# An FFT and two MLPs on one core: the start is folded by VectorE alone, weights are made one unit ahead, rows of tiles lie 1664 bytes apart

## The chip, the core and the metric

One core of a Trainium2 chip runs the program. The metric is the time of one execution on the device in microseconds; lower is better. It is given as the median of a few runs, and one execution more was recorded by the hardware profiler.

## What is computed

The reference takes `x` (4 batches, 3072 tokens, 256 columns), makes the real part of a 2D Fourier transform of each batch, and passes every token through two MLPs:

```python
X = np.fft.fft(np.fft.fft(x, axis=1), axis=2).real
h = X @ w_in;  g = np.maximum(0.01 * h, h);  y = g @ w_out          # 256 -> 2048 -> 256
xk, xr = mixes of y and of y one token earlier, by mu_k and mu_r
k = np.maximum(xk @ w_k, 0);  out = sigmoid(xr @ w_r) * (k * k @ w_v)  # 256 -> 1024 -> 256
```

The weights arrive as 64-bit floats.

## The kernel before

**Two parts.** The first part makes `y`, the second (from about 950 us on) makes the output. Matmuls of precision run as three: each operand is split into a high and a low part, and high x high, high x low and low x high are added (`hi_lo`, line 80: ScalarE copies the high part, VectorE subtracts to get the low part).

**Folding and the transform along tokens.** The transform along the columns is taken into `w_in` (below), so that only the tokens are transformed. Rows of `x` come in six groups of 128 partitions with four mirrored rows each (`xl`, 512 KB a group). Sums and differences of the mirrored rows and columns (`full`, lines 187 to 197, for batch 0; DMAs that add, `second`, and `fin` for batches 1 to 3) give `plus` and `minus`, which hold four operands: "Pe", "Qe", "Po" and "Qo". Each is multiplied with two tables (`fft_a`, line 233, with the first three groups, `fft_b`, line 245, with the last three); between the two halves ScalarE copies the first half's sum (`ev`), and from both VectorE makes two of the four classes of frequencies A1, A2, G1, G2. A class has 386 or 384 columns; its P part is even and its Q part odd in the columns. One column apart from the others (column 128) goes the same way in small: `c_fold`, `c_a`, `c_b`; its row goes out to DRAM (`cd`) and comes back spread over all partitions (`load_c`, tile `cb`).

**Units.** For each batch, class and 128 columns of `w_in`'s 2048 there is a unit, 16 units a class, 4 x 4 x 16 = 256 in all. `mm_a` (line 476) multiplies the P part with the even weights `weh`, `wel`; `ev_a` (484) on VectorE adds the row `cb` times `w128`; `mm_b` (489) adds the Q part with `woh`, `wol`; VectorE makes `d`, ScalarE the two leaky results `g`, ScalarE and VectorE split them into `gh` and `gl`, and `outmm` (496) does twelve matmuls with `w_out`. `step` (536) issues `mm_b` of this unit, `mm_a` of the next, and `outmm` of the unit two before. After `step`, the functions that the loop calls are queued behind it on their engines: the order of the program text is the order of each engine's queue.

**Weights.** A quarter-megaword piece of 64-bit weights (256 columns of `w_in`, or 256 rows of `w_out`) is turned into 32-bit floats with a correction in three steps (`f64_steps`, line 95): ScalarE `h`, VectorE two operations, VectorE one more, ScalarE `lf`, and a product on GpSimd (`r`). `w_in_mm` (310) multiplies a piece of `w_in` with cosine and sine matrices, `w_in_split` (324) splits it (ScalarE `wh`, VectorE `wl`), `w_in_row` (333) makes `w128`. For `w_out` the steps are named `wout[q][0]` (those three), `[1]` (ScalarE copy, GpSimd sum) and `[2]` (VectorE `uol`). In the kernel before, pieces 0 to 2 of `w_in` and 0 and 1 of `w_out` are taken up before the first unit, and the others in `boot` (457) while units 0 to 11 run, each two or three units before it is used.

**The start.** Lines 394 to 454 are the order before the first unit. Groups 0, 1, 3 and 4 are folded by VectorE and groups 2 and 5 by GpSimd. All loads are issued from SyncE's queue (SP) in this order: `w_in` 0, `ce`, `so`, row groups 0, 2, 1, `w_in` 1, five small loads, row groups 5, 3, 4, tables a, b, `w_out` 0, tables a2, b2, further weights.

Of the kernel before, what the change touches and what calls it, by code (L numbers as in the profile page):

```python
# [55 lines left out]
def fft_mlp_kernel(ctx, tc, xa, xb, x7, x8, x87, tb, alt, ce, so, mu, w_in, w_out, w_k, w_v, w_r, out):  # L56
# [104 lines left out]
    def fold_ops(b):  # L161
# [5 lines left out]
        def first(g, p=None):  # L167
            if b == 0:
                t = st[g] = p.tile([P, 2, 2, D], F32, tag="xl", bufs=2 if p is fft else 4, name=f"xl{b}_{g}")
                Q.dma_start(t[:, 0], xa[b, g])  # L170
                Q.dma_start(t[:, 1], xb[b, g, :, :, 0:D])
            else:
                eo[g] = fft.tile([P, 2, 2, P], F32, tag="eo", bufs=2, name=f"eo{b}_{g}")
                st[g] = fft.tile([P, 2, D], F32, tag="xl", bufs=2, name=f"xl{b}_{g}")
                Q.dma_start(eo[g][:, 0], xa[b, g, :, :, 0:P])
                Q.dma_start(st[g], xa[b, g])


        def second(g):
            E = eo[g][:, 0]  # L180
            G.dma_start(E, xa[b, g, :, :, P:D], accum_op=ALU.add)
            G.dma_start(st[g], xb[b, g, :, :, P:P + D], accum_op=ALU.add)
            G.dma_start(E, xb[b, g, :, :, 0:P], accum_op=ALU.add)
            G.dma_start(E, xb[b, g, :, :, P:D], accum_op=ALU.add)


        def full(g, E, tags):
            t = st[g].rearrange("p z o d -> p (z o) d")
            e = work.tile([P, 4, P], F32, tag=tags[0][0], bufs=tags[0][1], name=f"fe{g}")
            o = work.tile([P, 4, P], F32, tag=tags[1][0], bufs=tags[1][1], name=f"fo{g}")  # L190
            eo[g] = work.tile([P, 2, 2, P], F32, tag=tags[2][0], bufs=tags[2][1], name=f"eo{b}_{g}")
            E.tensor_tensor(e, t[:, :, :P], t[:, :, P:], op=ALU.add)  # L192
            E.tensor_tensor(o, t[:, :, :P], t[:, :, P:], op=ALU.subtract)  # L193
            E.tensor_tensor(eo[g][:, 0], e[:, 0:2], e[:, 2:4], op=ALU.add)  # L194
            E.tensor_tensor(eo[g][:, 1], o[:, 0:2], o[:, 2:4], op=ALU.subtract)
            fin(g, 2, E)
            fin(g, 3, E)
# [21 lines left out]

        return first, second, full, fin, load7, fold7  # L220
# [24 lines left out]
    def fft_b(b, kind, ps, ev):
# [5 lines left out]
        y1 = pqp.tile([P, JP], F32, tag=nm, bufs=3, name=f"c{b}{kind}1")  # L251
        y2 = pqp.tile([P, JP], F32, tag=nm, bufs=3, name=f"c{b}{kind}2")
        act_copy(y1, ps[:, :JP])
        if nm == "P":
            V.scalar_tensor_tensor(y2, ev, 2.0, y1, op0=ALU.mult, op1=ALU.subtract)
        else:
            V.scalar_tensor_tensor(y2, ev, -2.0, y1, op0=ALU.mult, op1=ALU.add)

            for k, y in ((k1, y1), (k2, y2)):
                if b == 0 and k == A1:  # L260
                    act_copy(y[0:1], cs0[0:1, 0])
                else:
                    Q.dma_start(y[0:1], cd[b, k:k + 1])
# [80 lines left out]
    def w_out_load(q, ahead=False):  # L344
        if q < 8:
            st = load_f64(w_out[q * 256:(q + 1) * 256].rearrange("(k p) d -> p k d", p=P), 2, D, ahead)
            s = slice(2 * q % HF, 2 * q % HF + 2)
            wout[q] = f64_hi_lo(uoh[2 * q // HF][:, s], uol[2 * q // HF][:, s], st, 2, D, *((work, "gl") if q < 3 else (stage, "f")))


    def c_fold():
# [56 lines left out]
    next_tabs(2)
    w_out_load(0)
    next_tabs(2)  # L410
    w_in_load(2, True)
    w_out_load(1, True)
    w_in_load(3)
    w_out_load(2)
    w_in_parts(0)
# [19 lines left out]
    w_in_split(1)
    wout[0][0]()
    pe = fft_a(0, "Pe")
    ca = c_a(c8p, "a", True)
    w_in_row(1)
    w_in_parts(2)  # L440
    fft_b(0, "Pe", *pe)
    wout[0][1]()
    cs0 = c_b(c8p, "b", A1, *ca)
    cur_c = load_c(0, A1)
    wout[1][0]()
    qe = fft_a(0, "Qe")
    wout[0][2]()
# [559 lines left out]
```

## Time and profile before

| | us |
|---|---|
| median of 3 runs | 1550.82 |
| lowest and highest | 1550.01, 1552.66 |
| the profiled execution | 1551.64 |
| its span, first to last instruction | 1549.8 |
| TensorE (PE) busy | 1518.3 |
| VectorE (DVE) busy | 1065.6 |
| ScalarE (ACT) busy | 917.5 |
| GpSimd (POOL) busy | 162.0 |

The engines work side by side, each through its own queue, and wait for one another by semaphores. The chain of waits that ended last is followed back from the end of the program; what stands in it sets the time. TensorE's clock is gated: the profile lists the granted clock (1.0 is 2.4 GHz, 0.5 is 1.2 GHz).

### The profile page before, as it was taken

The numbers are of one execution on the slowest core, as the hardware profiler recorded it, in microseconds if no ns is written. First come the engines' busy times: TensorE is split into PE (matmuls) and PEld (weight loads), VectorE is DVE, ScalarE is ACT, GpSimd is POOL, SyncE is SP. The second block draws the span as 40 slices with busy tenths as digits, with TensorE's granted clock in tenths as the row PEclk, the third lists the DMA queues.
The fourth block names the chain that finished last, engine by engine and source line by source line (L and its number), as shares of the span: only waits on it lengthen the run. The fifth ranks groups of instructions, "written<-read, shape, count | busy, mean of one in ns | idle before, by whom it ended". The sixth has DMA issues, their size and how long they took to land.

```text
span 1549.8 us, 22458 instructions
## 1 busy us (share of the span) xinstructions
PE 1518.3 (98%) x8418; PEld 1472.9 (95%) x8418; DVE 1065.6 (69%) x1783; ACT 917.5 (59%) x1761; POOL 162.0 (10%) x144
## 2 busy tenths in 40 slices
PE   5999999999999999999999999999999999999999
PEld 2789998999998999999999999999999999999998
DVE  7876775566766567666677775777777766777775
ACT  2565655556565555555566566666666666666664
POOL 4333210031200122100010000000000000000000
PEclk8999999999999999999999999999999999999999
DMA  7426312363312353212311001111111111111100
GB/s 246 154 73 138 77 31 80 106 136 63 75 26 90 105 117 53 56 42 74 107 53 28 19 21 42 41 52 50 48 48 41 42 42 41 42 42 42 42 21 32
DMA packets 74296, 102.12 MB, mean 66 GB/s; under 512 B 10798, under 2 KB 53822, under 8 KB 74186
## 3 DMA queue, kind: packets, MB, share of 16 engines
q1 hardware_dynamic: 54538, 88.85, 18.3%
q0 software_dynamic: 19648, 11.83, 5.9%
q8 instruction: 66, 1.08, 0.3%
q14 instruction: 44, 0.36, 0.1%
HBM read 72.83 MB, written 27.83 MB: 65 GB/s over the span
## 4 chain that ended last, share of the span: by engine, by line
PE 94%; DVE 2%; DMA 2%; issue 1%; ACT 1%; SPq 0%; POOL 0%; DVEq 0%; POOLq 0%; ACTq 0%
PE o L505 33%; PE kps L815 17%; PE v L856 17%; PE ps L494 8%; PE ps L482 8%; PE rps L864 4%; DMA xl<-in_xb 2%; PE wps L320 1%; PE cps L362 0%; DMA eo<-in_xa 0%; PE cps L371 0%; DVE fe L192 0%; DVE fo L193 0%; DVE ev L487 0%; DVE eo L194 0%
## 5 line engine op out<-in xcount | busy, mean ns | idle before, releaser
L546 DVE SCALAR_TENSOR_TENSOR d<-ev,ps 128x384 f32<-128x384 f32 (+1 forms) x256 | 141.8, 554 | 214.1 <-PE ps L494 213.9
L75 ACT ACTIVATE gh<-g 128x768 fp32r<-128x768 f32 (+1 forms) x256 | 216.6, 846 | 78.8 <-PE o L505 76.5
L819 ACT ACTIVATE rl<-kps 128x384 f32<-128x384 f32 x254 | 125.0, 492 | 218.5 <-PE kps L815 218.4
L526 DVE TENSOR_TENSOR gl<-g,gh 128x768 fp32r<-128x768 f32 (+1 forms) x256 | 250.8, 980 | 1.5 <-ACT gh L75 1.0
L78 ACT ACTIVATE g<-ps 128x384 f32<-128x384 f32 (+1 forms) x256 | 126.1, 492 | 211.3 <-DVE d L546 211.1
L820 DVE SCALAR_TENSOR_TENSOR k<-kps,rl 128x384 f32<-128x384 f32 x254 | 141.6, 558 | 137.8 <-ACT rl L819 133.9
L505 PE MATMUL o<-gl,uoh 128*128 128x384 f32 (+1 forms) x1024 | 229.9, 339 | 0.0
L505 PE MATMUL o<-gh,uoh 128*128 128x384 f32 (+1 forms) x1024 | 229.4, 338 | 0.0
L505 PE MATMUL o<-gh,uol 128*128 128x384 f32 (+1 forms) x1024 | 229.0, 337 | 0.0
L505 PEld LDWEIGHTS o<-gl,uoh 128*128 128x128 f32 x1024 | 184.0, 188 | 0.0
L505 PEld LDWEIGHTS o<-gh,uol 128*128 128x128 f32 x1024 | 184.0, 188 | 0.0
L505 PEld LDWEIGHTS o<-gh,uoh 128*128 128x128 f32 x1024 | 183.8, 188 | 0.0
L487 DVE SCALAR_TENSOR_TENSOR ev<-cb,w,ps 128x384 f32<-128x384 f32 (+1 forms) x256 | 157.2, 614 | 0.0
L82 DVE TENSOR_TENSOR k2l<-k,k2h 128x384 fp32r<-128x384 f32 x254 | 139.5, 549 | 0.4 <-ACT k2h L75 0.4
L856 PE MATMUL v<-k2h,wvh 128*128 128x384 f32 x510 | 135.1, 336 | 0.0
L856 PE MATMUL v<-k2h,wvl 128*128 128x384 f32 x510 | 135.1, 336 | 0.0
L856 PE MATMUL v<-k2l,wvh 128*128 128x384 f32 x510 | 135.1, 336 | 0.0
L78 ACT ACTIVATE g<-d 128x384 f32<-128x384 f32 (+1 forms) x256 | 132.9, 519 | 0.0
L75 ACT ACTIVATE k2h<-k 128x384 fp32r<-128x384 f32 x254 | 131.2, 517 | 0.0
L815 PE MATMUL kps<-mh,wkh 128*128 128x384 f32 x508 | 129.6, 336 | 1.3 <-ACT mh L75 0.7
L815 PE MATMUL kps<-ml,wkh 128*128 128x384 f32 x508 | 129.5, 336 | 0.0
L815 PE MATMUL kps<-mh,wkl 128*128 128x384 f32 x508 | 129.4, 336 | 0.0
(295 smaller groups left out, 2497.5 us busy)
## 6 DMA issues: line engine op xcount, KB each, us to landing
out_dram<-o SPq DMA_DIRECT2D x31, 384.0 KB
y<-yo SPq DMA_DIRECT2D x24, 384.0 KB
xl<-in_xa SPq DMA_DIRECT2D x24, 256.0 KB
xa<-y SPq DMA_DIRECT2D x16, 384.0 KB
tab_a<-in_tb SPq DMA_DIRECT2D x8, 579.0 KB
tab_b<-in_tb SPq DMA_DIRECT2D x8, 579.0 KB
tab_c<-in_tb SPq DMA_DIRECT2D x8, 579.0 KB
tab_d<-in_tb SPq DMA_DIRECT2D x8, 579.0 KB
```

The costliest lines, as they stand in the source:

```text
L75: A.activation(o, i, ACTF.Copy)
L78: A.activation(o, i, ACTF.Prelu, alpha=0.01)
L82: V.tensor_tensor(lo, src, hi.bitcast(F32), op=ALU.subtract)
L482: T.matmul(x["ps"][:, :n], l[:, f], r[:, :n], start=(i == 0), stop=(i == 2))
L487: V.scalar_tensor_tensor(x["ev"][:, :n], x["cb"][:, :n], w128[:, u:u + 1], x["ps"][:, :n], op0=ALU.mult, op1=ALU.add)
L505: T.matmul(po[s][h][:, :n], w[:, u % HF, h * P:(h + 1) * P], g[:, s, :n], start=(u == 0 and i == 0), stop=(u == NF - 1 and i == 2))
L526: V.tensor_tensor(gl[:, :, :n], x["g"][:, :, :n], x["gh"][:, :, :n].bitcast(F32), op=ALU.subtract)
L546: V.scalar_tensor_tensor(d[:, :n], x["ev"][:, :n], 2.0, x["ps"][:, :n], op0=ALU.mult, op1=ALU.subtract)
L815: T.matmul(ps[:, :J], w[:, k, sl], x[:, k], start=(i == 0), stop=(i == 5))
L819: A.activation(r, ps[:, :J], ACTF.Relu)
L820: V.scalar_tensor_tensor(k2, ps[:, :J], 0.0, r, op0=ALU.max, op1=ALU.mult)
L856: T.matmul(vps[m][:, :J], w[:, f, m * P:(m + 1) * P], x, start=(f == 0 and i == 0), stop=(f == NK - 1 and i == 2))
```

## The change

- Batch 0 is folded by VectorE alone, each group in three parts: `even0` (sums, and `plus` for "Pe"), `odd0` (differences, and `minus` for "Qe"), and `rest0` ("Po" and "Qo"), which runs after unit 1. The differences overwrite the rows in place. A group comes with one load (`x0`) instead of two.
- The order of loads: row groups 0 to 2, table a, row groups 3 to 5, table b, `w_in` 0, tables a2 and b2, `w_in` 1, `w_out` 0. Six small loads are issued from ScalarE's queue. Four `memset`s go from VectorE to GpSimd, and `c_b`'s write to DRAM goes from GpSimd's queue to SyncE's.
- Before the first unit only piece 0 of `w_in` is made ready, and piece 1 between `mm_a` and `mm_b` of unit 0. `boot` makes the others over units 0 to 15, each one unit before use; `w_in_row` stands inside `step`, between `mm_b` and the next `mm_a`. The halves of A2 that come from "Pe" and "Qe" (`later`) are made after unit 0. `fft_a` of "Po" goes from unit 2 to unit 5, the small `c_a` and `c_b` one unit later.
- Tiles with rows of 386 columns (1544 bytes) get rows of `PJ` = 416 columns (1664 bytes), of which 386 or 384 are used.

```diff
+PJ = 416
...
+        def even0(g):
+            if g % 3 == 0:
+                sums.append(work.tile([P, 3, 2, P], F32, tag="yo", bufs=2, name=f"sums{g}"))
+            t, E = st[g], sums[g // 3][:, g % 3]
+            e = work.tile([P, 4, P], F32, tag="g", bufs=2, name=f"fe{g}")
+            V.tensor_tensor(e, t[:, :, :P], t[:, :, P:], op=ALU.add)
+            V.tensor_tensor(E, e[:, 0:2], e[:, 2:4], op=ALU.add)
+            V.tensor_tensor(plus[:, g, 0], E[:, 0], E[:, 1], op=ALU.add)
+
+        def odd0(g):
+            t = st[g]
+            o = work.tile([P, 4, P], F32, tag="gh", bufs=2, name=f"fo{g}")
+            O = eo[g] = t[:, 0].rearrange("p (o n) -> p o n", o=2)
+            V.tensor_tensor(o, t[:, :, :P], t[:, :, P:], op=ALU.subtract)
+            V.tensor_tensor(O, o[:, 0:2], o[:, 2:4], op=ALU.subtract)
+            V.tensor_tensor(minus[:, g, 1], O[:, 0], O[:, 1], op=ALU.subtract)
+
+        def rest0(g):
+            if g % 3 == 0:
+                E = sums[g // 3]
+                V.tensor_tensor(minus[:, g:g + 3, 0], E[:, :, 0], E[:, :, 1], op=ALU.subtract)
+            V.tensor_tensor(plus[:, g, 1], eo[g][:, 0], eo[g][:, 1], op=ALU.add)
+            if g == 0:
+                fold7o()
...
-    V.memset(one0.bitcast(F32), 0.0)
-    V.memset(one0[0:1].bitcast(F32), 1.0)
-    V.memset(altt, 0.0)
-    V.memset(e7p, 0.0)
+    G.memset(altt, 0.0)
+    G.memset(e7p, 0.0)
+    G.memset(one0.bitcast(F32), 0.0)
+    G.memset(one0[0:1].bitcast(F32), 1.0)
...
-        G.dma_start(cd[:, k1:k1 + 2], cs)
-        return cs
+
+        def other():
+            V.scalar_tensor_tensor(cs[:, 1], ev, 2.0, ps[:4, :JP], op0=ALU.mult, op1=ALU.subtract)
+            Q.dma_start(cd[:, k1:k1 + 2], cs)
+        return cs, other
...
+    A.dma_start(x8t, x8)
+    A.dma_start(x87t, x87)
+    A.dma_start(altt[0:1], alt)
+    load7(A)
+    A.dma_start(cet, ce)
+    A.dma_start(sot, so)
     act_copy(cer, cet)
     act_copy(sor, sot)
+    for g in range(3):
+        load0(g, rows if g else fft)
+    next_tabs(1)
+    for g in range(3, 6):
+        load0(g, fft if g == 3 else rows)
+    next_tabs(1)
+    w_in_load(0)
+    next_tabs(2)
+    w_in_load(1)
+    w_out_load(0)
+    c_fold()
+    fold7e()
+    for g in range(3):
+        even0(g)
+    ca = c_a(c8p, "a", True)
+    pe = fft_a(0, "Pe")
+    odd0(0)
+    for g in range(3, 6):
+        even0(g)
+    cs0, c_other = c_b(c8p, "b", A1, *ca, "gl")
+    w_in_parts(0)
+    later = []
+    fft_b(0, "Pe", *pe, later)
+    odd0(1)
+    c_other()
+    cur_c = load_c(0, A1)
+    cur = split_class(0, A1, "P")
     w_in_mm(0)
...
+    odd0(2)
+    qe = fft_a(0, "Qe")
     w_in_split(0)
...
     w_in_row(0)
...
+    for g in range(3, 6):
+        odd0(g)
+    fft_b(0, "Qe", *qe, later)
+    cur += split_class(0, A1, "Q")
+    w_in_load(2)
     next_tabs(2)
...
+    def rest(u):
+        if u == 0:
+            for g in later:
+                g()
+        if u == 1:
+            for g in range(6):
+                rest0(g)
+            rows.release()
...
     def boot(u):
         q = u // 2
         if u % 2 == 0:
...
+            w_in_split(q + 1)
+            if q < 8:
+                wout[q][1]()
+            w_in_parts(q + 2)
+            w_in_load(q + 3)
         else:
...
+            wout[q][2]()
+            if q < 7:
+                wout[q + 1][0]()
+            w_in_mm(q + 2)
+            w_out_load(q + 2)
...
-        x["ev"] = work.tile([P, JP], F32, tag="as", bufs=2, name="ev")
+        x["ev"] = work.tile([P, PJ], F32, tag="as", bufs=2, name="ev")
...
-        gh = work.tile([P, 2, JP], F32R, tag="gh", bufs=2, name="gh")
+        gh = work.tile([P, 2, PJ], F32R, tag="gh", bufs=2, name="gh")
...
             mm_b(x)
+            if x["b"] == 0 and x["c"] == A1 and x["u"] % 2:
+                w_in_row(x["u"] // 2 + 1)
...
     nx = unit(0, A1, 0, cur, cur_c)
     mm_a(nx)
     ev_a(nx)
-    w_in_split(2)
-    wout[1][2]()
+    wout[0][0]()
+    w_out_load(1)
+    next_tabs(2)
+    w_in_parts(1)
+    w_in_mm(1)
...
-        po_u, qo_u, f0, f1 = (2, 10, 17, 52) if b == 0 else (0, 3, 8, 52)
+        po_u, qo_u, f0, f1 = (5, 10, 17, 52) if b == 0 else (0, 3, 8, 52)
```

All other tiles of 386 columns (`fv`, the classes and their high and low parts, `cb`, `yo`, `gl`, `d`, `g`) change their row as `ev` and `gh` do.

## Rows read from the trace of the kernel before

**Rows 1.** The page: the span, section 1's line of the two parts of TensorE, DVE, ACT and POOL (busy us, share, instructions), and section 2's line of the granted TensorE clock in 40 equal slices of the span, in tenths of full speed.

```profile
span 1549.8 us, 22458 instructions
...
PE 1518.3 (98%) x8418; PEld 1472.9 (95%) x8418; DVE 1065.6 (69%) x1783; ACT 917.5 (59%) x1761; POOL 162.0 (10%) x144
...
PEclk8999999999999999999999999999999999999999
```

**Rows 2.** Stretches of 10 us at the start: length, then busy us and number of instructions of PE, PEld, DVE, ACT and POOL, the mean granted clock, the DMA share and GB/s.

```profile
20.00:30.00 10.00, 7.06 (x24) 4.46 (x23) 9.90 (x17) 1.79 (x4) 7.57 (x7) 0.82 0.99 380
...
40.00:50.00 10.00, 7.18 (x28) 4.57 (x27) 8.84 (x14) 5.19 (x11) 5.66 (x5) 1.00 0.54 190
...
60.00:70.00 10.00, 9.76 (x47) 7.82 (x47) 8.65 (x14) 6.33 (x14) 3.90 (x3) 1.00 0.40 125
```

**Rows 3.** TensorE in order of time over the first 75 us: start, length, engine, line, operation, output and inputs, count, and in brackets the idle time before it with what ended it (Q stands for the classes of odd columns; L494 is the second half of a unit, L482 the first).

```profile
24.01 2.19 PE L238 MATMUL f0Pe<-tab_a,plus 128*128 128x386 f32 x6
...
29.99 3.54 PE L362 MATMUL cps<-tab_a,c8p 128*4 128x386 f32 x6
...
34.84 2.19 PE L249 MATMUL f0Pe<-tab_b,plus 128*128 128x386 f32 x6
...
43.85 1.03 PE L320 MATMUL wps<-fv,cet 128*128 128x256 f32 x4
...
45.62 0.59 PE L322 MATMUL wps<-r,sor 128*128 128x256 f32 x2
...
49.51 0.41 PE L494 MATMUL ps<-Qh,wh 128*128 128x386 f32 x1 [1.55 <-DVE ev L487]
...
50.65 0.17 PE L340 MATMUL wps<-one,wh 128*128 128x2 f32 x1
...
70.13 0.63 PE L494 MATMUL ps<-Qh,wh 128*128 128x386 f32 x1
```

**Rows 4.** VectorE (DVE) in order of time over the first 75 us, same columns.

```profile
5.41 0.43 DVE L102 TENSOR_SCALAR h<-h 128x512 uint32<-128x512 uint32 x1 [3.87 <-ACT h L100]
...
7.61 1.39 DVE L192 TENSOR_TENSOR fe<-xl 128x512 f32<-128x512 f32 x1 [0.59 <-DMA xl<-in_xb]
...
29.22 0.67 DVE L192 TENSOR_TENSOR fe<-xl 128x512 f32<-128x512 f32 x1
...
30.42 0.41 DVE L194 TENSOR_TENSOR eo<-fe 128x256 f32<-128x256 f32 x1
...
31.20 0.43 DVE L203 TENSOR_TENSOR plus<-eo 128x256 f32<-128x256 f32 x1
...
40.86 0.69 DVE L108 SCALAR_TENSOR_TENSOR fv<-st,h 128x512 uint32<-128x512 uint32 x1
...
46.72 0.56 DVE L82 TENSOR_TENSOR Pl<-c0Pe,Ph 128x386 fp32r<-128x386 f32 x1 [1.01 <-ACT Ph L75]
...
48.76 0.60 DVE L487 SCALAR_TENSOR_TENSOR ev<-cb,w,ps 128x386 f32<-128x386 f32 x1
...
50.48 0.54 DVE L546 SCALAR_TENSOR_TENSOR d<-ev,ps 128x386 f32<-128x386 f32 x1
...
73.61 0.95 DVE L526 TENSOR_TENSOR gl<-g,gh 128x772 fp32r<-128x772 f32 x1
```

**Rows 5.** ScalarE (ACT) in order of time over the first 75 us, same columns.

```profile
4.72 0.66 ACT L100 ACTIVATE h<-st 128x512 f32<-128x512 f32 x1 [2.70 <-DMA st<-in_w_in]
...
45.75 0.53 ACT L75 ACTIVATE c0Qe<-cs 1x386 f32<-1x386 f32 x1 [1.21 <-DVE c0Qe L257]
...
46.60 0.51 ACT L75 ACTIVATE Qh<-c0Qe 128x386 fp32r<-128x386 f32 x1
```

**Rows 6.** GpSimd (POOL) in order of time over the first 75 us, same columns.

```profile
7.16 1.29 POOL L115 TENSOR_TENSOR r<-st,h 128x512 fp32r<-128x512 f32 x1 [6.71 <-DVE h L111]
```

**Rows 7.** The DMA view of the first 70 us: GB/s in 40 slices of 1.75 us, and one group of issues (output, input, queue, count, KB, us from issue to landing).

```profile
GB/s 0 193 354 382 353 373 244 270 230 353 341 374 426 412 400 386 325 14 0 0 0 5 0 5 11 118 305 411 418 401 349 62 82 221 0 12 297 108 97 202
...
cd<-cs POOLq DMA_DIRECT2D x1, 12.1 KB, 2.1
```

**Rows 8.** The chain that ended last, 120 to 180 us: start, length, engine, output, line, count (twelve matmuls of L505 are one unit's products with the second matrix).

```profile
125.52 0.54 PE ps L494 x3
...
126.58 2.12 PE o L505 x12
...
142.41 2.12 PE o L505 x12
...
145.59 2.11 PE o L505 x12
...
174.04 2.10 PE o L505 x12
```

**Rows 9.** The same chain, 1190 to 1230 us, where groups of six matmuls follow each other.

```profile
1190.31 1.04 PE kps L815 x6
...
1225.67 1.04 PE kps L815 x6
```

**Rows 10.** Groups of instructions by line with different shapes apart: engine, operation, output and inputs, shape, count, busy us, mean ns of one, idle time before.

```profile
L505 PE MATMUL o<-gh,uoh 128*128 128x384 f32 x768 | 172.0, 338 | 0.0
...
L856 PE MATMUL v<-k2h,wvh 128*128 128x384 f32 x510 | 135.1, 336 | 0.0
...
L482 PE MATMUL ps<-Ph,wh 128*128 128x384 f32 x192 | 65.0, 338 | 0.0
```

More of the change, by code (lines that the diff above doesn't have):

```diff
@@ L165, in fold_ops, with first @@
         st, eo = {}, {}
[L167 to L176, printed above, removed]
+        def first(g):
+            eo[g] = fft.tile([P, 2, 2, P], F32, tag="eo", bufs=2, name=f"eo{b}_{g}")
+            st[g] = fft.tile([P, 2, D], F32, tag="xl", bufs=2, name=f"xl{b}_{g}")
+            Q.dma_start(eo[g][:, 0], xa[b - 1, g, :, :, 0:P])
+            Q.dma_start(st[g], xa[b - 1, g])
         def second(g):
             E = eo[g][:, 0]
[L181 to L197, printed above, removed]
+            G.dma_start(E, xa[b - 1, g, :, :, P:D], accum_op=ALU.add)
+            G.dma_start(st[g], xb[b - 1, g, :, :, P:P + D], accum_op=ALU.add)
+            G.dma_start(E, xb[b - 1, g, :, :, 0:P], accum_op=ALU.add)
+            G.dma_start(E, xb[b - 1, g, :, :, P:D], accum_op=ALU.add)
         def fin(g, q, E=V):
@@ L214, in fold7, with fold7o @@
+        def fold7o(E=V):
+            t = st["x7"]
             o7 = fft.tile([1, 2, P], F32, tag="o7", bufs=1, name=f"o7_{b}")
-            E.tensor_tensor(e7, t[:, :, :P], t[:, :, P:], op=ALU.add)
             E.tensor_tensor(o7, t[:, :, :P], t[:, :, P:], op=ALU.subtract)
-            E.tensor_tensor(e7p[0:1], e7[:, 0], e7[:, 1], op=ALU.add)
             E.tensor_tensor(plus[0:1, 0, 1], o7[:, 0], o7[:, 1], op=ALU.subtract)
-        return first, second, full, fin, load7, fold7
+        sums = []
@@ L222, in fft_mlp_kernel @@
+        if b == 0:
+            return load0, even0, odd0, rest0, load7, fold7e
+        return first, second, fin, load7, lambda: (fold7e(G), fold7o(G))
     folded, classes = {}, {}
@@ L250, in fft_b, with row0 @@
         nm = kind[0]
[L251 to L255, printed above, removed]
-        else:
[L257 to L263, printed above, removed]
+        y1 = pqp.tile([P, PJ], F32, tag=nm, bufs=3, name=f"c{b}{kind}1")
+        y2 = pqp.tile([P, PJ], F32, tag=nm, bufs=3, name=f"c{b}{kind}2")
+        act_copy(y1[:, :JP], ps[:, :JP])
+        def row0(k, y):
+            if nm == "Q":
+                if b == 0 and k == A1:
+                    act_copy(y[0:1, :JP], cs0[0:1, 0])
+                else:
+                    Q.dma_start(y[0:1, :JP], cd[b, k:k + 1])
+        def other():
+            s, op = (2.0, ALU.subtract) if nm == "P" else (-2.0, ALU.add)
+            V.scalar_tensor_tensor(y2[:, :JP], ev[:, :JP], s, y1[:, :JP], op0=ALU.mult, op1=op)
+            row0(k2, y2)
+        if later is None:
+            other()
+            row0(k1, y1)
+        else:
+            row0(k1, y1)
+            later.append(other)
         classes[b, nm, k1] = y1
@@ L408, in fft_mlp_kernel @@
[L408 to L415, printed above, removed]
+    load0, even0, odd0, rest0, load7, fold7e = fold_ops(0)
+    G.memset(c87, 0.0)
+    A.dma_start(x8t, x8)
[4 more added lines that the diff above has]
+    A.dma_start(sot, so)
     act_copy(cer, cet)
     act_copy(sor, sot)
+    for g in range(3):
+        load0(g, rows if g else fft)
@@ L435, in fft_mlp_kernel @@
[L435 to L447, printed above, removed]
-    next_tabs(2)
-    w_in_parts(3)
-    wout[1][1]()
-    fft_b(0, "Qe", *qe)
-    next_tabs(2)
-    cur = split_class(0, A1, "P") + split_class(0, A1, "Q")
-    w_in_mm(2)
+    w_in_row(0)
+    for g in range(3, 6):
+        odd0(g)
```

108 lines of the change are left out of this document (40 added, 68 removed).

## The prediction

> **What bounds the kernel now.** I read the page first, to see that TensorE is busy for 1518.3 of 1549.8 us and that its clock is full from the second slice on [rows 1]. Nothing after the start can be gained except by taking TensorE work away or making each matmul shorter, so the questions are two: where TensorE loses time in the first units, and whether its matmuls run as short as they can. The 10 us stretches answer the first: 7.06 of 10 us busy at clock 0.82 in 20 to 30, 7.18 in 40 to 50, 9.76 in 60 to 70 [rows 2]. From there I went to each engine's own timeline [rows 3 to 6] and to the loads [rows 7]; the marks are unit 0's second half (`mm_b`) at 49.51, unit 4's at 70.13 [rows 3], and unit 16's, the first of the second class, at 125.52 [rows 8]. After unit 16 both kernels have the same TensorE work left, so the change of the start is worth the shift of unit 16. For the second question the chain is read: 15 units from 126.58 to 174.04 are 3.164 us each [rows 8], while 34 groups of six matmuls of the same width from 1190.31 to 1225.67 are 1.04 us each, 3.12 for 18 [rows 9]. A unit is 18 matmuls, so each unit is 0.044 us longer than it would be at the pace of the second part.
>
> **The start, step by step.** Durations are of the rows; an operation's successor on its engine starts some 0.07 us before its listed end.
>
> Folding. With GpSimd at work (7.16, 1.29 us [rows 6]) a sum of 512 elements takes VectorE 1.39 us (7.61), without it 0.67, and 256 elements 0.41 [rows 4]. Alone, VectorE needs for `even0` or `odd0` of a group 0.60 + 0.34 + an estimated 0.22 (half of the 0.43 for 256) = 1.16 us. Six of each are 14 us.
>
> Loads. A first 512 KB had landed by 4.72 [rows 5]; after it 353 to 382 GB/s flow [rows 7], 0.36 MB/us. In the new order that puts row groups 0 to 2 at 8.5 (1.57 MB and 0.31 MB of small loads), table a (0.59 MB) at 10.1, groups 3 to 5 at 14.5, table b at 16.1, `w_in` 0 at 17.6, a2 and b2 at 19.2 and 20.9. `even0` of group 5 ends at 15.7.
>
> TensorE to table b. It starts at 10.1 with `c_a`. Six table matmuls took 3.54 us at 29.99 and 2.19 at 24.01 and 34.84 [rows 3], at a low and at the full clock; with the two matmuls of the extra row I take 4.7 for `c_a` and 2.8 for the half of "Pe": 17.5. `c_b` follows to 19.6, a ScalarE copy to 20.1.
>
> Here the first wait of the new order stands. In ScalarE's queue the first step of `w_in` 0 (0.66 [rows 5]) is behind that copy, so VectorE, whose queue has `w_in_parts(0)` next, is idle from 15.7 to 20.8; `odd0(1)`, `odd0(2)` and all that follows are queued behind it. Then three operations (0.43, 0.69 [rows 4] and 0.43 again) to 22.3, `odd0(1)` beside a GpSimd product to 24.3, `c_other` and `Pl` (0.56 [rows 4]) to 25.4, `odd0(2)` to 26.6. TensorE does half of "Qe" to 28.7; ScalarE its copy and only then `wh`: 29.8; VectorE `wl` to 30.5 and `odd0` 3 to 5 to 34.0. The other half of "Qe" ends at 36.1 (at the low clock 37.5), three ScalarE copies (0.53, 0.51 [rows 5]) at 37.6 to 39.0, `Ql` and `ev` (0.60 [rows 4]) at 38.8 to 40.2. Before `mm_b(0)` TensorE's queue holds `w_in_mm(1)`: two preparations on VectorE (1.55 each), a product on GpSimd (1.29 [rows 6]) and what is left of 2.36 us of matmuls (43.85 to 45.62 + 0.59 [rows 3]). `mm_b(0)` comes at 45 to 47 instead of 49.51.
>
> Units 0 to 4. VectorE's work from there to unit 4's `ev`: four `d` and four `ev` (0.54 + 0.60) 4.6; two `gl` (0.95 [rows 4]) 1.9; two `wl` and one `uol` 2.1; three preparations 4.6; the two `later` 1.1; `rest0` 3.1 (two of 384 elements, six of 128, two small). That is 17.4. Stretches beside seven GpSimd operations of 1.3 us add 2 to 3, waits for ScalarE's copies 2 to 4; I take 22.5. `mm_b(4)` is then at 69 (65 to 72), against 70.13. But at its unit 4 the old kernel had five pieces of `w_in` multiplied, four `w_in_row` done and all of "Po"; the new one has four, three and none. That is 2.36 + 0.4 (four small matmuls from 50.65 [rows 3]) + 2 x 2.05 = 6.9 us of TensorE work more. From 70.13 to 125.52 the old one took 55.4; the new one gets to unit 16 at 69 + 55.4 + 6.9 = 131.3. **The start costs 6 us**, 2 to 9 by the bounds of unit 4.
>
> What costs nothing, and by which cover: the `memset`s on GpSimd (idle until the first product), the small loads from ScalarE (idle until 4.72; needed from 10 on), the write of `cd` from SyncE. The last adds a wait: SyncE stands until `c_other` at 24.8, 2.1 us pass to the landing [rows 7], and `load_c`, `w_in` 2 and tables c, d are queued behind; `cb` is there by 30 and `w_in` 2 by 33, both needed after 38. Without those 5 us the first unit would move by as much. Two fewer groups on GpSimd are worth nothing by themselves, since its later products wait for VectorE.
>
> **Rows 1664 bytes apart.** The bounds are rows. At best all of the 0.044 us goes: 256 x 0.044 = 11.3 us gained. At worst every unit becomes like the longest one shown (142.41 to 145.59, 3.18 [rows 8]): 4 us lost. Between: matmuls on `g`'s parts average 338 ns, and so do those on the P class, whose 386 columns begin at the start of a tile of their own, against 336 in the second part [rows 10]. So the excess is not confined to tiles with a second row, and the new distance changes less than it would if it were. I take a quarter of the best, **2.5 us gained**.
>
> A page of the Trainium skill, "SBUF — State Buffer", section "Door 1: The DMA port swizzle", says that SBUF is read in lines of 16 bytes and that each access crossing to a new line pays. 1544 bytes are 96.5 such lines and 1664 are 104; by that rule the second rows of `gh`, `gl` and `g` begin in the middle of a line now and no longer do so after. No row here shows the price; the P class rows just named speak against it as the only cause. By it, the full 11.3 us would be the term.
>
> **The sum.** 1551.64 (the profiled execution, 1.84 above its span) + 6 - 2.5 = 1555.1; the median of the runs is 0.82 lower than that execution, so 1554.3.
>
> **Rivals.**
> 1. The spacing pays in full (-11.3) and the start costs 6: 1550.8 - 5.3 = 1545.5. For it: the second part, where every row distance is 1536 bytes, has the shorter pitch throughout. Against it: the P class. Chance 0.14.
> 2. The start comes early. VectorE's own work from 15.7 to unit 4 sums to about 30 us, so that unit 4 could come at 46 if nothing waited; I forecast 23 us of waits and stretches. If it is 14 (TensorE at the full clock from its second table on, GpSimd's products falling beside operations that are not stretched), unit 4 comes at 60 and unit 16 at 122.3: -3.2 - 2.5, 1545.1. This decides for faster from unit 4 at 62 on. For it: in the old kernel VectorE was the engine most held up by GpSimd. Against it: the waits are in the order of the queues. Chance 0.16.
> 3. The two terms nearly cancel (unit 4 at 65 to 67, or half of the spacing's best): 1548 to 1553.9. Chance 0.23.
> 4. One unit ahead is too late: `w_in_row` stands in TensorE's queue between `mm_b` and `mm_a` of every second unit and waits for `wl`, behind `d`, `ev` and `gl` on VectorE. From 0.5 us of such a wait for six pairs on it adds 3 us and more to the forecast: 1557 to 1561. Before, the same matmuls stood behind `outmm` and an extra unit. Chance 0.12.
>
> **How the numbers follow.** The forecast itself has 0.35, with 1552 to 1558 as its own range. A measurement here tells 0.2% (3.1 us) from no change: faster is below 1547.7, slower above 1553.9. Rivals 1 and 2 are faster, 0.30; rival 3 the same, 0.23; the forecast and rival 4 slower, 0.47. The range 1545 to 1561 leaves out the ends of rivals 1, 2 and 4.
>
> **What would show it.** In the new profile: VectorE idle from about 16 to 21; `mm_b(0)` at 45 to 47; TensorE idle between units 2 and 3 while VectorE does `rest0`; `mm_b(4)` near 69 and unit 16 near 131; a unit of 3.15 us in place of 3.164. It is wrong if unit 16 starts before 125.5, or if the matmuls' pitch falls to that of the second part.

## The result

The changed kernel takes 1575.6 us (median of 4 runs, 1572.5 to 1576.7) where the kernel before takes 1550.9: 1.0149 times as long, with an interval from 1.0135 to 1.0164. Measured again later (experiment 16) it took 1572.0 against 1552.2 (1.0122, 1.0105 to 1.0138). The forecast was 1554.3, its range ended at 1561. The direction was right, the size was not.

Where the time went is read from the start of each unit's second half (`mm_b`), before and after:

| `mm_b` of unit | before | after | later by |
|---|---|---|---|
| 0 | 49.51 | 47.66 | -1.85 |
| 4 | 70.13 | 74.02 | 3.89 |
| 12 | 112.34 | 121.88 | 9.54 |
| 14 | 118.98 | 129.33 | 10.35 |
| 15 | 122.17 | 144.50 | 22.33 |
| 16 | 125.36 | 148.39 | 23.03 |
| 72 | 319.32 | 341.67 | 22.35 |
| 80 | 347.05 | 371.03 | 23.98 |
| 136 | 540.99 | 564.33 | 23.34 |
| 144 | 569.28 | 595.84 | 26.56 |
| 255, the last | 937.44 | 962.60 | 25.16 |

There are four terms. **The start** costs 10.35 us, up to unit 14. **One hole** between units 14 and 16 costs 12.7, which the forecast did not contain. **Units** are shorter, by 3.2 us from 16 to 255. **Waits in the folds of batches 2 and 3** (units 72 to 80 and 136 to 144) are 5.3 longer in this profile; how these last two are kept apart is told at experiments 10 and 12. The sum is 25.2. The first three belong to the change. The fourth differs from run to run: in a second profile of the same kernel (16) it is 2.7, and no run shows that the change makes it. The start moves between runs too: in the eight profiles of kernels with its order up to there, unit 0 comes between 46.00 and 48.62.

### The profile page after: what moved, and what is told of

Its sections match the earlier page's. It is cut to its first block, busy times and chain, and to the rows that moved or that the text cites. A ratio compares the mean times of both kernels' runs of the same rounds, so it can differ in the third digit from the quotient of the medians.

```text
span 1574.7 us, 22455 instructions
## 1 busy us (share of the span) xinstructions
PE 1523.3 (97%) x8418; PEld 1474.8 (94%) x8418; DVE 1065.2 (68%) x1798; ACT 916.0 (58%) x1761; POOL 147.1 (9%) x135
## 4 chain that ended last, share of the span: by engine, by line
PE 88%; DMA 2%; DVE 1%; ACT 0%; issue 0%; SPq 0%; POOL 0%; DVEq 0%; POOLq 0%; ACTq 0%
PE o L538 31%; PE kps L855 17%; PE v L896 17%; PE ps L527 8%; PE ps L515 8%; PE rps L904 4%; DMA xl<-in_xb 1%; DMA xl<-in_xa 0%; DVE ev L520 0%; DMA eo<-in_xa 0%; DVE d L581 0%; PE ps L855 0%; DVE wl L134 0%; PE f1Qe L270 0%; PE f3Qe L270 0%
## 5 line engine op out<-in xcount | busy, mean ns | idle before, releaser
L538 PE MATMUL o<-gh,uol 128*128 128x384 f32 (+1 forms) x1024 | 230.8, 340 | 10.5 <-DVE uol L134 10.5
L538 PE MATMUL o<-gh,uoh 128*128 128x384 f32 (+1 forms) x1024 | 230.9, 340 | 0.0
L538 PE MATMUL o<-gl,uoh 128*128 128x384 f32 (+1 forms) x1024 | 229.6, 338 | 0.0
L538 PEld LDWEIGHTS o<-gh,uol 128*128 128x128 f32 x1024 | 185.0, 190 | 10.8 <-DVE uol L134 10.8
L538 PEld LDWEIGHTS o<-gh,uoh 128*128 128x128 f32 x1024 | 184.5, 190 | 0.0
L538 PEld LDWEIGHTS o<-gl,uoh 128*128 128x128 f32 x1024 | 183.9, 189 | 0.0
```

The costliest lines, as they stand in the source:

```text
L538: T.matmul(po[s][h][:, :n], w[:, u % HF, h * P:(h + 1) * P], g[:, s, :n], start=(u == 0 and i == 0), stop=(u == NF - 1 and i == 2))
```

## The profile after

The page: span, engines, granted clock in 40 slices, and the costliest group of TensorE that has an idle time.

```profile
span 1574.7 us, 22455 instructions
...
PE 1523.3 (97%) x8418; PEld 1474.8 (94%) x8418; DVE 1065.2 (68%) x1798; ACT 916.0 (58%) x1761; POOL 147.1 (9%) x135
...
PEclk9898999999999999999999999999999999999999
...
L538 PE MATMUL o<-gh,uol 128*128 128x384 f32 (+1 forms) x1024 | 230.8, 340 | 10.5 <-DVE uol L134 10.5
```

Against [rows 1], no engine was given more work: TensorE has the same 8418 matmuls, and the others are busy no longer. The span grew by idle time and by a lower clock, at which TensorE is busy for 5.0 us more; the clock is below full in two slices instead of one. The last line names the new wait: 10.5 us, once, for `uol`, the low part of a piece of `w_out`. L538 is L505 of before; L527 is L494, L515 is L482.

Stretches of 10 us, columns as in [rows 2], and a fourth one where the hole is:

```profile
20.00:30.00 10.00, 8.49 (x29) 4.14 (x27) 6.08 (x11) 2.83 (x6) 1.61 (x1) 1.00 0.21 75
...
40.00:50.00 10.00, 5.73 (x20) 4.47 (x21) 4.98 (x8) 2.06 (x5) 3.87 (x3) 0.66 0.59 207
...
60.00:70.00 10.00, 4.69 (x15) 4.18 (x16) 9.46 (x19) 4.85 (x11) 3.46 (x3) 0.71 0.16 52
130.00:140.00 10.00, 1.23 (x8) 0.91 (x6) 0.00 (x0) 0.34 (x1) 2.48 (x3) 0.79 0.66 150
```

From 20 to 30 the new order is better than [rows 2] (8.49 for 7.06). From 40 to 50 VectorE has work for half the time and yet TensorE waits for it; from 60 to 70 VectorE is full and TensorE waits. From 130 to 140 VectorE does nothing at all, and GpSimd has three instructions.

TensorE in order of time, columns as in [rows 3]:

```profile
43.56 2.08 PE L351 MATMUL wps<-fv,cet 128*128 128x256 f32 x4 [5.85 <-DVE fv L109]
...
47.66 0.34 PE L527 MATMUL ps<-Qh,wh 128*128 128x386 f32 x1
...
58.74 0.86 PE L538 MATMUL o<-gl,uoh 128*128 128x386 f32 x4
65.02 0.69 PE L527 MATMUL ps<-Qh,wh 128*128 128x386 f32 x1 [5.42 <-DVE ev L520]
...
68.63 1.49 PE L538 MATMUL o<-gh,uoh 128*128 128x386 f32 x4
...
74.02 0.34 PE L527 MATMUL ps<-Qh,wh 128*128 128x386 f32 x1
...
141.77 1.65 PE L538 MATMUL o<-gh,uol 128*128 128x386 f32 x4 [10.53 <-DVE uol L134]
...
144.50 0.52 PE L527 MATMUL ps<-Qh,wh 128*128 128x386 f32 x1
```

Three holes are of the change: 5.85 us for piece 1 of `w_in`, 5.42 for unit 3's `ev`, 10.53 for `uol`. Each costs more than its idle time, since the clock is low behind it: four matmuls that take 0.86 us at 58.74 take 1.49 at 68.63 and 1.65 at 141.77, and the four at 43.56 take 2.08, where the kernel before needed 1.03 [rows 3].

VectorE over the same time, columns as in [rows 4]:

```profile
22.52 0.43 DVE L103 TENSOR_SCALAR h<-h 128x512 uint32<-128x512 uint32 x1 [5.73 <-ACT h L101]
...
24.77 1.40 DVE L228 TENSOR_TENSOR xl<-fo 128x256 f32<-128x256 f32 x1
...
28.05 0.43 DVE L228 TENSOR_TENSOR xl<-fo 128x256 f32<-128x256 f32 x1
...
30.82 0.69 DVE L361 TENSOR_TENSOR wl<-wps,wh 128x512 fp32r<-128x512 f32 x1 [2.02 <-ACT wh L76]
...
59.51 1.38 DVE L235 TENSOR_TENSOR plus<-xl 128x128 f32<-128x128 f32 x1
...
68.96 0.61 DVE L520 SCALAR_TENSOR_TENSOR ev<-cb,w,ps 128x386 f32<-128x386 f32 x1
...
141.02 0.69 DVE L134 SCALAR_TENSOR_TENSOR uol<-r,uoh 128x512 fp32r<-128x512 f32 x1 [12.02 <-POOL r L130]
```

It is idle from 16.8 to 22.5 behind ScalarE's copy of `c_b`, and for 12.02 us ahead of `uol`, which waits for GpSimd. So the last view is GpSimd's queue, columns as in [rows 6]:

```profile
120.05 1.30 POOL L116 TENSOR_TENSOR r<-st,h 128x512 f32<-128x512 f32 x1 [3.76 <-DVE h L112]
126.98 1.23 POOL L177 DMA_DIRECT2D eo<-in_xa  x1 [5.64 <-DMA eo<-in_xa]
128.11 1.24 POOL L178 DMA_DIRECT2D xl<-in_xb  x1
134.94 1.09 POOL L179 DMA_DIRECT2D eo<-in_xb  x1 [5.59 <-DMA eo<-in_xa]
138.61 1.08 POOL L180 DMA_DIRECT2D eo<-in_xb  x1 [2.58 <-DMA eo<-in_xb]
139.36 1.62 POOL L130 TENSOR_TENSOR r<-r,fv 128x512 f32<-128x512 f32 x1
```

The four DMAs are `second(0)` of batch 1, which add rows in place; each onto the same tile waits until the one ahead has landed. They are issued after unit 11. From the end of the product at 121.35 the queue stands, first 5.64 us for the plain loads of those rows, then for the DMAs themselves. The sum behind them (139.36) belongs to piece 6 of `w_out`, which `boot` issues after unit 12. It needs nothing of the DMAs; it merely stands behind them in the queue. In the kernel before the same queue had them the other way round, the last sum (L129) ahead of the DMAs:

```profile
109.63 1.87 POOL L129 TENSOR_TENSOR r<-r,fv 128x512 f32<-128x512 f32 x1
117.39 1.14 POOL L181 DMA_DIRECT2D eo<-in_xa  x1 [5.89 <-DMA eo<-in_xa]
...
124.93 1.08 POOL L183 DMA_DIRECT2D eo<-in_xb  x1 [5.27 <-DMA eo<-in_xa]
128.66 1.07 POOL L184 DMA_DIRECT2D eo<-in_xb  x1 [2.65 <-DMA eo<-in_xb]
```

A page of the Trainium skill, "DMA: Bandwidth & Descriptors", section "Rules for kernel authors", says that an adding DMA next to another access of the same bytes must wait for that one's semaphore; the waits of 5.59 and 2.58 us, and of 5.27 and 2.65 in the kernel before, are what this costs here.

The chain of waits (start, length, engine, output, line, count) gives the length of a unit:

```profile
155.95 2.10 PE o L538 x12
...
203.25 1.92 PE o L538 x11
```

Fifteen units in 47.30 us are 3.153 each, against 3.164 in [rows 8].

## Experiments

**Theory Q**: the hole behind unit 14 is GpSimd's queue, a sum standing behind DMAs that it does not need. **Theory O**: what is lost before unit 14 is lost by the order of the instructions in VectorE's and ScalarE's queues. Their rivals are that the DMAs' transfers hold up everything whatever stands in the queue, and **V**, that VectorE's amount of work sets the time of the start whatever its order. The terms of the other runs are spelled out with them. Unless another is named, an edit is to the changed kernel.

**1. The DMAs of batch 1 after the last sum.**

```diff
-                        second(0)
+                        if b > 0:
+                            second(0)
...
+                if b == 0 and i == 14:
+                    second(0)
...
-        po_u, qo_u, f0, f1 = (5, 10, 17, 52) if b == 0 else (0, 3, 8, 52)
+        po_u, qo_u, f0, f1 = (5, 10, 20, 52) if b == 0 else (0, 3, 8, 52)
```

> The changed kernel, with the four adding DMAs of batch 1's first fold group issued after unit 14 instead of unit 11 (and its first fold step at unit 20 instead of 17). Theory Q: the 10.5 us hole of TensorE at 131 to 141 is GpSimd's queue, where the sum of w_out piece 6 stands behind those DMAs; it goes, unit 15 starts near 132.5 instead of 144.5, and the time falls by 10 to 12 us to 1564. Rival D: the piece's data or the memory traffic is late, not the queue; then the hole stays and the time is 1575.

1560.0 us (1.0057, 1.0042 to 1.0072), 15.5 less than the changed kernel. GpSimd and TensorE in order of time:

```profile
121.14 1.28 POOL L130 TENSOR_TENSOR r<-r,fv 128x512 f32<-128x512 f32 x1
...
134.21 1.22 POOL L177 DMA_DIRECT2D eo<-in_xa  x1
```

```profile
129.04 0.34 PE L527 MATMUL ps<-Qh,wh 128*128 128x386 f32 x1
132.20 0.34 PE L527 MATMUL ps<-Qh,wh 128*128 128x386 f32 x1
135.35 0.34 PE L527 MATMUL ps<-Qh,wh 128*128 128x384 f32 x1
```

The sum runs at 121.14, 18.2 us earlier than behind the DMAs, and units 14 to 16 follow each other at 3.15 us. The hole is gone: 13.0 us at unit 16. In the profiles the rest lies in the folds of batches 2 and 3, whose waits differ from run to run; against the changed kernel of experiment 16 the time is 12.0 us less.

**6. The same DMAs where they were, but the two last sums and one product on VectorE.**

```diff
-            G.tensor_tensor(z["r"], z["r"], z["f"], op=ALU.add)
+            z.get("S", G).tensor_tensor(z["r"], z["r"], z["f"], op=ALU.add)
```

The product changes likewise, with `"E"`; pieces 6 and 7 get VectorE.

> The changed kernel with the sum of w_out piece 6 and the product and sum of piece 7 on VectorE instead of GpSimd; batch 1's adding DMAs stay after unit 11. Theory Q (GpSimd's queue): unit 15 starts at 132 to 134 instead of 144.5, time 1561 to 1564. Rival D (the transfers at that time hold something up, whoever adds): the hole stays, 1573 or more.

1559.7 us (1.0041, 1.0026 to 1.0056). The DMAs run as late as in the changed kernel (127.43 to 139.98), and of the hole 0.70 us is left:

```profile
133.78 0.44 PE L527 MATMUL ps<-Qh,wh 128*128 128x386 f32 x1 [0.70 <-DVE ev L520]
```

So it is not the transfers that hold up the work but the queue. With 1 this settles theory Q.

**3. The order before the first unit.** Three steps move ahead: `w_in_parts(0)` in front of `c_b`, `w_in_parts(1)` in front of the second half of "Qe", `w_in_mm(1)` in front of `wout[0][0]`.

```diff
+    w_in_parts(0)
     cs0, c_other = c_b(c8p, "b", A1, *ca, "gl")
-    w_in_parts(0)
...
+    w_in_parts(1)
     fft_b(0, "Qe", *qe, later)
...
+    w_in_mm(1)
     wout[0][0]()
     w_out_load(1)
     next_tabs(2)
-    w_in_parts(1)
-    w_in_mm(1)
```

> The changed kernel with the preparation of w_in piece 0 ahead of c_b, and that of piece 1 ahead of the second half of Qe, so that VectorE does them in its idle times (5.7 us at 16.8, 3.2 us at 35.7). Theory O: the start lost by the order of the queues; unit 0 at 42 to 43 instead of 47.7, units 4 and on 4 to 5 us earlier, time 1570 to 1571. Rival V: VectorE's load sets the start; unit 0 is earlier but unit 4 is within 1 us of 74, time 1574 to 1576.

1566.1 us (1.0087, 1.0070 to 1.0104), 9.5 less than the changed kernel. TensorE (L528 is L527, L539 is L538):

```profile
37.45 0.34 PE L528 MATMUL ps<-Qh,wh 128*128 128x386 f32 x1
...
65.01 0.34 PE L528 MATMUL ps<-Qh,wh 128*128 128x386 f32 x1
```

```profile
132.15 1.65 PE L539 MATMUL o<-gh,uol 128*128 128x386 f32 x4 [9.95 <-DVE uol L134]
```

Unit 0 comes 10.2 us earlier (37.45 for 47.66), unit 4 9.0 (65.01 for 74.02), and unit 14 still 9.0 (120.29 for 129.33), with the same work on each engine. That is theory O, and more than was expected of it. The hole for `uol` stays.

**4. `later` and `rest0` moved on, two groups a unit in units 2 to 4.**

```diff
-        if u == 0:
+        if u == 3:
...
-        if u == 1:
-            for g in range(6):
-                rest0(g)
+        if u in (2, 3, 4):
+            rest0(2 * u - 4)
+            rest0(2 * u - 3)
+        if u == 4:
```

> The changed kernel with the rest of the fold spread over units 2 to 4 (two groups each) instead of after unit 1, and the two halves of class A2 after unit 3 instead of unit 0. Theory O: the 5.4 us hole of TensorE before unit 3 mostly goes; unit 3 at 59 to 61 instead of 65, unit 10 three to five us earlier, time 1571. Rival V: VectorE is the bound to unit 5 in either order; unit 5 is within 1 us of 77.2 and the time 1574 to 1576.

1572.9 us (1.0138, 1.0123 to 1.0153). TensorE:

```profile
58.61 0.34 PE L528 MATMUL ps<-Qh,wh 128*128 128x386 f32 x1
...
73.54 0.63 PE L528 MATMUL ps<-Qh,wh 128*128 128x386 f32 x1 [4.55 <-DVE ev L521]
```

```profile
84.62 0.63 PE L528 MATMUL ps<-Qh,wh 128*128 128x386 f32 x1
```

The hole before unit 3 is gone (58.61 for 65.02), another of 4.55 us stands before unit 5, and unit 6 at 84.62 is where it was (84.65). The hole was moved, and the time is that of the changed kernel in experiment 16 within 1 us. Neither forecast is met to the letter: unit 5 is 3.7 us earlier (73.54 for 77.19), where rival V had it unmoved, but unit 10 comes where it was (109.26 for 109.30), where theory O had a gain. In substance V is right here: in this order VectorE's work up to unit 6 is the bound, and it has to be done by then.

**5. 1 and 3 together.**

> The changed kernel with both edits of before: batch 1's adding DMAs after unit 14, and the preparations of w_in 0 and 1 earlier in the queues. If the two losses are separate, they add: 1560.0 - 9.5 = 1550.5. If the second only hides in the first, 1555 or more.

1553.5 us (1.0004, 0.9994 to 1.0014): the two causes are most of the loss. Unit 16 comes at 127.10, 1.7 us later than in the kernel before. There the two gains add, as the first forecast had it: 21.3 us together, 13.0 and 8.8 apart. The time lies between the two forecasts, and in this profile the fold waits cost 10.4 us, as in the changed kernel's.

**7. 5 and 4, and `w_in_split(0)` in front of `odd0(2)` and the first half of "Qe".**

> As e5_late_order, and w_in_split(0) ahead of odd0(2) and Qe's first half (2 us of VectorE's idle time at 26), and the rest of the fold over units 2 to 4. Theory: where VectorE is no longer held up, the later rest gives something too: unit 12 three to five us earlier than in the order run, time 1546 to 1549, under the kernel before. Rival V: VectorE's work up to unit 5 is the bound; unit 12 within 1 us of 112.9, time 1550 to 1552.

1550.9 us (0.9987, 0.9974 to 1.0001). The time is the rival's, the start is not: unit 12 comes at 110.19, 2.7 us earlier than in 3 (112.85), nearly what the theory asked for. Unit 16 is now 1.4 us ahead of the kernel before, unit 255 1.5 behind it in this profile: the fold waits again (11.2 us).

**2. The kernel before with rows of 416 columns, nothing else** (each `JP` of a tile's row becomes `PJ`, as in the change's diff).

> The kernel before with rows 1664 bytes apart and nothing else. Theory: a unit becomes 3.1535 us as in the changed kernel (3.164 before), 256 units make -2.7 us: 1548. Rival 1: the shorter unit belongs to other things in the changed kernel, time 1551. Rival 2: it is worth the full 11 us where the start does not hide it: 1540.

1551.2 us (0.9994, 0.9985 to 1.0004, 10 runs): no difference to be told, as rival 1 had it, although its profile has unit 255 2.8 us earlier, as the theory had it. Runs of this kernel lay 5 us apart, which asked for their cause.

**9. Experiment 1 with rows of 386 columns** (`PJ = 386`).

> As e1_late_second, with rows 1544 bytes apart again. If the distance is worth what the unit pitch says (0.0105 us x 256), the time is 1560.0 + 2.7 = 1562.7 and the unit pitch is back at 3.164; if it is worth nothing, 1560.

1558.7 us (1.0039, 1.0024 to 1.0054), the same as experiment 1 within what can be told. Units 19 to 47 take 88.46 us against 88.29 there and 88.62 in the kernel before, units 16 to 72 193.47 against 193.29 and 193.96. Between half and three quarters of the gain is in the changed kernel without the wider rows.

**10, 11, 12. The folds of batches 2 and 3 taken up three units later** in the changed kernel (10), in 7 (11) and in the kernel before (12).

```diff
-        po_u, qo_u, f0, f1 = (5, 10, 17, 52) if b == 0 else (0, 3, 8, 52)
+        po_u, qo_u, f0, f1 = (5, 10, 17, 52) if b == 0 else (0, 3, 11, 52)
```

> The changed kernel with the fold of batches 2 and 3 begun at unit 11 instead of 8 and nothing else. If the holes at 348 and 570 (2.3 and 3.7 us) are waits for the adding DMAs of a fold that begins too early, both go and the time is 1569 to 1570; if the DMAs themselves are slower after the change, the waits come at a later step and the time is 1574 to 1576.

> The best start of the run before (rest over units 2 to 4), with the fold of batches 2 and 3 begun at unit 11: 1550.9 less the two holes of 2.6 and 3.7 us, 1544 to 1546. Rival (the waits move to a later step): 1550 to 1551.

> The kernel before with the fold of batches 2 and 3 begun at unit 11 and nothing else. Its holes at 325 and 547 are 2.2 and 2.7 us: 1546 to 1547 if they go, 1551 if they move. Against this the versions with the changed start show what the start itself is worth.

1565.8 us (1.0095, 1.0080 to 1.0110), 1542.8 (0.9947, 0.9932 to 0.9962) and 1546.3 (0.9969, 0.9958 to 0.9981), and the runs of each lie within 2 us. Experiment 12 meets its forecast; 10 and 11 come out 3.2 and 1.2 us lower, since the forecasts took the idle time alone, and the waits cost more than that. Unit 8 of a batch is where VectorE takes up a tile that those adding DMAs fill, and at 11 it has landed. Set against these kernels, unit by unit, the folds of batches 2 and 3 cost 4.1 and 6.3 us in the changed kernel's profile and 2.3 and 2.8 in that of before. Most of the difference is the clock. VectorE's wait in the fold of batch 2, TensorE's behind it, and stretches of 3 us around them, first of the changed kernel, then of the kernel before:

```profile
348.96 0.42 DVE L184 TENSOR_TENSOR eo<-xl 128x256 f32<-128x256 f32 x1 [4.55 <-DMA xl<-in_xb]
350.44 0.44 PE L527 MATMUL ps<-Qh,wh 128*128 128x386 f32 x1 [2.30 <-DVE ev L520]
348.00:351.00 3.00, 0.70 (x4) 0.57 (x4) 2.04 (x4) 1.12 (x3) 0.38 (x1) 0.98 0.43 66
351.00:354.00 3.00, 3.00 (x11) 3.00 (x10) 2.75 (x5) 1.85 (x4) 2.92 (x3) 0.50 0.42 50
```

```profile
326.38 0.42 DVE L201 TENSOR_TENSOR eo<-xl 128x256 f32<-128x256 f32 x1 [4.31 <-DMA xl<-in_xb]
327.86 0.45 PE L494 MATMUL ps<-Qh,wh 128*128 128x386 f32 x1 [2.00 <-DVE ev L487]
326.00:329.00 3.00, 1.14 (x6) 1.14 (x7) 2.62 (x5) 1.69 (x4) 1.46 (x3) 1.00 0.32 40
329.00:332.00 3.00, 3.00 (x19) 3.00 (x18) 2.54 (x6) 2.13 (x4) 1.83 (x2) 1.00 0.83 94
```

After an idle time of 2.30 us the clock is at 0.50, its low level of 1.2 GHz, and 11 matmuls run in 3 us; after 2.00 it stays at 1.00 and 19 run. TensorE's wait is 0.30 us longer, and the fold costs 1.9 us more. But the length of a wait does not decide alone whether the clock falls. The wait in batch 3 of the kernel before, behind which the clock stays at 1.00, and one of experiment 16 with the stretch behind it, at 0.51:

```profile
550.09 0.44 PE L494 MATMUL ps<-Qh,wh 128*128 128x386 f32 x1 [2.56 <-DVE ev L487]
```

```profile
348.37 0.45 PE L527 MATMUL ps<-Qh,wh 128*128 128x386 f32 x1 [2.02 <-DVE ev L520]
349.00:352.00 3.00, 3.00 (x11) 3.00 (x11) 3.00 (x6) 1.79 (x4) 2.42 (x3) 0.51 0.61 75
```

Over the twelve profiles of kernels that take up the fold at unit 8, the two waits cost from 4.6 us (experiment 3) to 11.2 (experiment 7), and the changed start is at both ends. What decides this in a run is not settled.

Without these waits the changed kernel is 1565.8 - 1546.3 = 19.5 us slower, and the terms say 10.35 + 12.7 - 3.2 = 19.85.

**8. All of it**: 7 with one group of `rest0` a unit in units 2 to 7 and the late folds.

> The best start of the run before with the rest of the fold one group a unit over units 2 to 7, and the fold of batches 2 and 3 begun at unit 11 of the batch instead of 8. Theory: TensorE's 4.5 us hole before unit 6 shrinks by 2 to 3, and the two holes of 2.6 and 3.7 us where VectorE waits for the adding DMAs of batches 2 and 3 go: 1541 to 1545. Rival: VectorE's work only moves, and the DMA waits come at a later step of the fold: 1549 to 1552.

1542.4 us (0.9943, 0.9928 to 0.9958), ahead of both kernels, 3.9 us ahead of experiment 12. In the profiles 1.1 us are there at unit 16, the rest is the shorter unit. That is the forecast, but the late fold gives it: against 11, which has it too, spreading the rest further is worth 0.3 us of time, less than can be told. The hole shrank by 0.7 us only, from 4.56 in 7; it stands before unit 5, the sixth unit:

```profile
61.73 0.45 PE L528 MATMUL ps<-Qh,wh 128*128 128x386 f32 x1 [3.87 <-DVE ev L521]
```

**13 to 16. The rows again, with the fold waits gone, and why these grew.** 13 is 2 with the late folds, 14 is 8 with `PJ = 386`, 15 is the changed kernel with `PJ = 386`, 16 the changed kernel unchanged.

> The kernel before with rows of 416 columns and f0 of batches 1 to 3 at unit 11, so that no fold waits are left. Theory L (the wider rows pay 2.7 us in the units, but lengthen the waits for the adding DMAs by about as much, which hid it when they were tried alone): 1546.3 - 2.7 = 1543.6, and the profile's unit 255 some 2.7 us earlier than that of the kernel before with the late fold. Rival N (the wider rows pay nothing in the time of the whole): 1546.3.

> The fastest kernel so far (reordered start, rest0 spread, late folds) with rows of 386 columns. Theory L: 1.5 to 2.7 us slower than with 416 columns (1542.4), so 1544 to 1545. Rival N: 1542.4, the same.

> The changed kernel with rows of 386 columns, nothing else. Theory L: units cost 1.5 to 2.7 us more, the fold waits of batches 2 and 3 fall from 9.8 to about the 4.8 of the kernel before: 1572.5 to 1574, at or below the changed kernel. Theory S (the fold waits grew with the later start, not with the rows): 1577 to 1578.3.

> The changed kernel once more, beside the one with rows of 386 columns on the same chip: both theories 1575.6, with the waits for the adding DMAs of batches 2 and 3 at about 10 us together, and the clock down to 0.50 behind each hole that is followed by it (those cost 4 to 6 us, the others 2.3 to 2.8).

13: 1543.6 us (0.9940, 0.9926 to 0.9955), 2.7 less than 12, as theory L had it, and its unit 255 is 2.9 us earlier. 14: 1543.5 (0.9938, 0.9926 to 0.9951), 1.1 more than 8, which the intervals do not tell apart; from unit 16 to unit 255 its profile is 1.1 us longer. So the wider rows are worth about 3 us in the kernel before and about 1 in the reordered one. 15: 1573.7 (1.0136, 1.0117 to 1.0155); 16: 1572.0 (1.0122, 1.0105 to 1.0138), less than expected. The time of 15 is theory L's, but not for its reason: narrow rows do not shorten the fold waits, which in the profiles cost 3.7 and 6.0 us in 15 and 3.9 and 3.9 in 16. That half of theory L falls, and theory S's time is not met either. In these runs (16) the changed kernel is 19.8 us above the kernel before, by the medians, which is what the first three terms give. Its two profiles lie 4.5 us apart at unit 255 (962.60 and 958.13): 1.8 of that is there at unit 16 (148.39 and 146.60, with unit 0 at 47.66 and 46.06), and 2.7 are the fold waits. What makes the start and these waits differ from one run to another is not settled.

## Why the prediction was wrong

**What bounds it, and unit 16 as the mark**: right in the main. 23.03 of the 25.16 us are there at unit 16. That the start is worth the shift of unit 16 and no more left out the waits in the folds: they put 5.3 us on this profile behind unit 16, of which the shorter units (3.2) hide a part.

**The start up to `mm_b(0)`**: right, and at most 0.7 us late. VectorE idle from 16.8 to 22.5 behind ScalarE's copy (forecast 15.7 to 20.8), `wl` at 30.8 (29.8 to 30.5), `mm_b(0)` at 47.66 (45 to 47).

**Units 0 to 4**: 5.0 us of the miss of 21.3. `mm_b(4)` came at 74.02, against 69 and the bounds 65 to 72. VectorE's path, which the forecast added up, came out: unit 4's `ev` is done at 69.57 (the row at 68.96). But TensorE was not ready for it. The hole between units 2 and 3 was foreseen; the matmuls that TensorE has to do between the hole and `mm_b(4)`, and the clock at which it does them, were not priced. From unit 3 to unit 4 9.00 us pass, and from 66 to 71 the granted clock is 0.50, with matmuls as long as in the row at 68.63.

**From unit 4 to 16**: this is the step that failed. It took the old 55.4 us and added 6.9 of TensorE work: 62.3. It took 74.4, which is 12.1 us of the miss. The 6.9 were nearly right (units 4 to 14 took 55.31 us for 48.85, 6.5 more). The other 12.7 us are the hole. The change moves the last pieces of `w_out` from before unit 12 to units 12 to 15. The forecast carried TensorE's moved work over, but did not follow those pieces through GpSimd's queue, where batch 1's DMAs stand from unit 11 on. "Two fewer groups on GpSimd are worth nothing by themselves, since its later products wait for VectorE" was all it said of that engine's later work. Experiments 1 and 6 show the queue as the cause: either way round it, the hole goes (but for 0.70 us in 6). With the 5.0 us of units 0 to 4 the term "the start costs 6 us" measured 23.0.

**The rows**: 2.5 us were forecast, a quarter of the best; 3.2 were seen from unit 16 on, and 2.7 in the time once the fold waits were gone (13 against 12). Unit pitch 3.15 was forecast, 3.153 measured. Had lines of 16 bytes, for each new one of which the Trainium skill ("SBUF — State Buffer", "Door 1: The DMA port swizzle") says an access pays, been the whole excess, 11.3 would have been gained: no run shows that. With rows of 1544 bytes the reordered kernel keeps 2.1 of the 3.2 us (14), so that lines crossed are at most a part of it. What else shortens a unit there was not tried.

**The rivals**: 1 did not occur. 2 asked for shorter waits on VectorE; the change does not have them, but three moved steps do (experiment 3), and even then unit 16 is not early while the DMAs stand in the queue. 3 did not occur. 4 was right that one unit ahead is late, but for the wrong weights: `w_in_row` waits for `wl` 0.76 us in unit 1, 0.29 in unit 3 and 0.12 in unit 13, TensorE for `w_out`'s `uol` once 10.53. The fold waits were in no rival; they stand in the trace of before as well, 5.1 us. The forecast's 0.35 was counted wholly as slower, though its own range began at 1552, below the 1553.9 where slower began.

## What to carry to other kernels

When work is moved to a later place, follow each instruction of it on each in-order queue, and look at what is queued there by then that waits for something else: here a sum of 1.3 us came 18 us late behind loads and DMAs that it did not need. Order in the queues counted for more than load: three moved steps gave 9.0 us (unit 14) and one moved group of DMAs 13.0 (unit 16), while work that was only put off moved its hole with it. A wait of 2 to 3 us on TensorE is worth removing for the clock behind it too: with the fold waits gone the runs of a kernel lay within 2 us of each other (10 to 12), with them up to 9 us apart (7). For the same reason a single profile is not enough to put such a wait down to a change.

## What the hardware showed

- A wait of TensorE can cost more than its idle time: in the changed kernel, behind idle times of 2.30, 3.72, 5.42 and 10.53 us, the clock was granted at about 0.5 and matmuls of 0.34 us took 0.52 to 0.53. Behind 2.00 and 2.56 us, in the kernel before, it stayed full. The length alone does not tell: in experiment 16 it fell behind 2.02 us.
- Four adding DMAs on GpSimd's queue hold up what is queued behind them for 12 us (126.98 to 139.36), of which the rows list GpSimd as busy for 4.6.
- Beside a GpSimd product some of VectorE's small operations lasted about as long as that product (1.36 to 1.61 us): 256 elements take 0.43 us alone and 1.40 beside it (28.05 and 24.77), 128 elements 1.38 (59.51). The Trainium skill, "SBUF — State Buffer", section "Who interferes with whom", says that a VectorE instruction with two inputs in SBUF contends with a GpSimd instruction that reads SBUF; these rows agree.
